# Loading wv in row blocks over two queues, and taking the v products of the first tiles block-complete

## The chip, the core and the metric

The kernel runs on one core of one Trainium2 chip. The metric is the device time in microseconds (us) of one execution; lower is better. The kernel before takes 220.84 us, the median of three runs (220.69, 220.84, 221.06).

## The reference, cut to what matters

The input x has 2048 rows of 512 numbers. It is normalised row by row, and the same normalised x feeds two branches whose results are added to x:

```python
xn = _layernorm(x)                       # no gain, no bias
q, k, v = split(xn @ wqkv)               # wqkv is 512 x 1536; 32 heads of 16
phi = concat(softmax(. @ w_phi), softmax(-(. @ w_phi)))      # for q and for k
o = (phi_q @ (phi_k^T v)) / (phi_q @ sum(phi_k) + 1e-6)      # per head
out = x + o @ wo + ((xn @ w_gate) * (xn @ w_up)) @ w_down    # inner width 1792
```

All inputs and the output are bf16. The change concerns v of the first 512 rows: `v = xn @ wv`, where wv is the last third (512 columns) of wqkv.

## The kernel before, in words

Rows of x are handled in 16 tiles of 128 rows; four tiles make a group of 512. wv lies in SBUF as four row blocks of 128 x 512 (`wv[:, c, :]`, 128 KB each); block c multiplies the 128 columns c of a tile, so a tile's v is four matmuls on TensorE (PE) that add up in one PSUM bank, one for each block, over the transposed tile (`xnT`) as the stationary operand. All matmuls of the start have 512 columns.

The order of the work on every engine is the order of the code (a manual schedule), and each engine works strictly in that order. The weights come by a list of transfers written out at the head of the kernel (lines 82 to 95): SyncE (SP) issues tile 0 of x, tile 2, wv blocks 0 and 1 in one transfer, wv blocks 2 and 3 in another, then the first 256 columns of the gate and up weights (`wg`, `wu`), `wphi`, the next 384 columns of `wg` and of `wu`, the transposed key weights (`wT2`), tiles 4 to 7 of x, and the rest. ScalarE (ACT) issues tiles 1 and 3 of x (lines 102 and 103). In the built program these transfers share eight semaphores that are handed out in turn, so a transfer is issued only after the one eight places before it (counted over both queues, in the order of the code) has landed. Before, `wphi` thus waits for tile 0, the second piece of `wg` for tile 2, the second piece of `wu` for wv blocks 0 and 1, `wT2` for tile 1, and tiles 4 to 7 for wv blocks 2 and 3.

The first four tiles are normalised in a special way, so that the start is short. For tile n, VectorE (DVE) sums the rows (`sum_of`, line 373; tile 1's sum is made on ACT, line 376), then writes 512 x minus the sum (`sub_sum`, line 337); the standard deviation is multiplied in only later, when v leaves PSUM (`first_v_out`, lines 361 and 363). `lt(n)` (lines 202 to 206) transposes the tile on PE with four matmuls of 128 columns against an identity and copies the result out of PSUM on ACT. `first_v(n, js)` (line 353, matmuls at line 236) makes the products of tile n with the wv blocks in js. Tiles 0 and 1 use the two banks that later hold the kv sums, tiles 2 and 3 ordinary banks (`pv`). `warm_up(k, reps)` (line 306) issues k matmuls on constants, of 128 x reps columns, which nothing reads.

Before, PE's order at the start (lines 380 to 397) is: ten constant matmuls, transposes of tiles 0 and 1, two constant matmuls of 512 columns, transposes of tile 2, then blocks 0 and 1 for tiles 0, 1 and 2 (six matmuls), transposes of tile 3, blocks 2 and 3 for tiles 0, 1 and 2 (six matmuls), all four blocks of tile 3. Then come three units of the gated branch (`ffn(3)`: four `g` matmuls at line 274, four `u` matmuls at line 278 each), `fold` (line 225), which multiplies the key weights by `w_phi` and needs `wT2` and `bd`, and from there the steady alternation of v, k, q, `ffn` and `kv`, the attention and the final products (`fin`, lines 290 and 293).

Of the kernel before, what the change touches and what calls it, by code (L numbers as in the profile page):

```python
# [8 lines left out]
BF16 = mybir.dt.bfloat16  # L9
F32 = mybir.dt.float32  # L10
AF = mybir.ActivationFunctionType
# [10 lines left out]
def kernel(  # L22
# [12 lines left out]
    nc = tc.nc  # L35
    P = 128
    S, D = A_x.shape[-2], A_x.shape[-1]
# [4 lines left out]
    DC = D // P  # L42
# [10 lines left out]
    consts = ctx.enter_context(tc.tile_pool(name="consts", bufs=1))  # L53
# [4 lines left out]
    wv = wpool.tile([P, DC, D], BF16)  # L58
# [9 lines left out]
    def dma_x(lo, hi, eng=nc.sync):  # L68
        eng.dma_start(out=xall[:, lo:hi, :], in_=x_view[:, lo:hi, :])
# [1 line left out]
    def dma_cols(eng, w, src, lo, hi, at=0):  # L71
        eng.dma_start(out=w[:, :, lo - at:hi - at], in_=src[:, lo:hi].rearrange("(c p) f -> p c f", p=P))

    def dma_wv(lo, hi):
        nc.sync.dma_start(out=wv[:, lo:hi, :],
                          in_=A_wqkv[lo * P:hi * P, 2 * D:3 * D].rearrange("(c p) f -> p c f", p=P))

    def dma_gu(lo, hi):
        dma_cols(nc.sync, wg, B_w_gate, lo, hi)
        dma_cols(nc.sync, wu, B_w_up, lo, hi)  # L80

    dma_x(0, 1)
    dma_x(2, 3)
    dma_wv(0, 2)
    dma_wv(2, DC)
    dma_gu(0, 2 * P)
    nc.sync.dma_start(out=wphi[:], in_=A_w_phi.rearrange("(c h) d f -> (h d) c f", c=DC))
    dma_gu(2 * P, 5 * P)
# [5 lines left out]
    nc.sync.dma_start(out=wd[:], in_=B_w_down.rearrange("(c p) d -> p c d", p=P))  # L94
    nc.sync.dma_start(out=wo[:], in_=A_wo.rearrange("(c p) n -> p c n", p=P))

    ET = mybir.EngineType
    ctx.enter_context(tc.manual_schedule(engines={ET.PE, ET.DVE, ET.Activation, ET.Pool, ET.SP}))
    ones = nc.const_aps.tensor(1.0, [P, P], BF16)
    first = consts.tile([P, 1], BF16)  # L100
    nc.scalar.activation(out=first[:], in_=ones[:, 0:1], func=AF.Exp, scale=1.0)
    dma_x(1, 2, nc.scalar)
    dma_x(3, 4, nc.scalar)
    ident = consts.tile([P, P], BF16)
    make_identity(nc, ident[:])
    mhalf = consts.tile([P, GT], F32)
# [38 lines left out]
    def bank(name, dt=F32, n=TT):  # L145
        return ps_s.tile([P, n], dt, name=name, tag="s")
# [55 lines left out]
    def lt(n, lo=0, hi=DC):  # L202
        tp = bank("tp", BF16).rearrange("p (c t) -> p c t", c=DC)
        for c in range(lo, hi):
            nc.tensor.transpose(out=tp[:, c, :], in_=xns[n][:, c * P:(c + 1) * P], identity=ident[:])  # L205
        nc.scalar.copy(out=xnT[:, lo:hi, n * P:(n + 1) * P], in_=tp[:, lo:hi, :])  # L206
# [27 lines left out]
    def proj(ps, n, w, js=range(DC)):  # L234
        for j in js:
            nc.tensor.matmul(ps, lhsT=xnT[:, j, n * P:(n + 1) * P], rhs=w[:, j, :],  # L236
                             start=(j == 0), stop=(j == DC - 1))
# [68 lines left out]
    def warm_up(k, reps=DC):  # L306
        for _ in range(k):
            nc.tensor.matmul(warm[:, 0:reps * P], lhsT=ones,
                             rhs=nc.const_aps.tensor(1.0, [P, reps * P], BF16), start=True, stop=True)
# [4 lines left out]
    with tc.tile_pool(name="ps_k", bufs=1, space=PSUM) as ps_k:  # L314
# [38 lines left out]
        def first_v(n, js):  # L353
            if n not in vps:
                vps[n] = kvbank[n][:] if n < 2 else bank("pv")
            proj(vps[n], n, wv, js)
# [23 lines left out]
        lt(0, 0, 2)  # L380
        lt(0, 2, DC)
        lt(1)
        warm_up(2)
        for n in (2, 3):
            sum_of(n)
            sub_sum(n, tots[n])
        lt(2)
        for n in range(3):
            first_v(n, (0, 1))
        lt(3)  # L390
        first_v(0, (2, 3))
        first_v(1, (2, 3))
        first_v(2, (2, 3))
        for n in (2, 3, 0, 1):
            stats_of(n)
            scales_of(n, float(D))
# [125 lines left out]
```

## Time and profile before

| what | value |
| --- | --- |
| median of three runs | 220.84 us (220.69 to 221.06) |
| the profiled execution's own time | 220.88 us |
| its span, first to last instruction | 219.1 us |
| PE busy | 215.2 us (98%) |
| DVE busy | 140.9 us (64%) |
| ACT busy | 89.4 us (41%) |
| GpSimd (POOL) busy | 74.1 us (34%) |
| moved by DMA | 19.91 MB, mean 91 GB/s |

The profile is one execution. Its span is 1.78 us shorter than that execution's own time; what lies around the span is taken as unchanged. In the rows, PE is the matmuls, PEld the loading of their stationary operands, SPq and ACTq the issuing of transfers. A busy time of PE includes the pipelined end of a matmul, so that single matmuls of 512 columns show 0.38 us though they follow one another about every 0.216 us (four of them take 0.86 us in the chain). A row of the timeline gives the start, the time covered, the engine, the line, the operation and how many of them; the chain that ended last gives start, length and what it consisted of. "To landing" counts from the start of an issue to the last part of the transfer.

### The profile page before, as it was taken

How to read it: one execution, taken by the hardware profiler on the slowest of the kernel's cores; microseconds unless marked ns; L12 is line 12 of the kernel's file. 1: busy time of each engine (PE TensorE's matmuls, PEld its weight loads, DVE VectorE, ACT ScalarE, POOL GpSimd, SP SyncE). 2: the span in 40 equal slices, each digit the busy share in tenths (PEclk: the TensorE clock that was granted, in tenths of full speed). 3: DMA queues.
4: the chain of work that ended last, by engine and by line, in shares of the span. 5: the costliest groups of instructions: out<-in, count | busy, mean ns of one | idle time of the engine just before them, and what ended most of it. 6: DMA issues, size and time to landing. Idle time of an engine off the chain costs nothing.

```text
span 219.1 us, 3493 instructions
## 1 busy us (share of the span) xinstructions
PE 215.2 (98%) x1294; PEld 103.1 (47%) x1294; DVE 140.9 (64%) x239; ACT 89.4 (41%) x159; POOL 74.1 (34%) x71
## 2 busy tenths in 40 slices
PE   8999999999999999999999999999999999999994
PEld 3444445454444444444544444444444444454443
DVE  4868867886598758567599773296655645454321
ACT  5545686569574875565435212141231322100000
POOL 2450843363358454636045333033123033000000
PEclk9999999999999999999999999999999999999999
DMA  6999995303202540202018455114431431612301
GB/s 193 276 298 372 373 242 50 75 0 51 48 0 49 51 85 11 48 3 48 1 37 102 80 112 114 42 24 96 96 75 24 96 72 27 97 48 72 74 24 48
DMA packets 48529, 19.91 MB, mean 91 GB/s; under 512 B 37504, under 2 KB 48512, under 8 KB 48512
## 3 DMA queue, kind: packets, MB, share of 16 engines
q1 hardware_dynamic: 48224, 19.42, 39.8%
q10 hardware_dynamic: 288, 0.26, 0.4%
q8 instruction: 10, 0.16, 0.4%
q14 instruction: 7, 0.06, 0.1%
HBM read 8.67 MB, written 2.10 MB: 49 GB/s over the span
## 4 chain that ended last, share of the span: by engine, by line
PE 96%; DVE 1%; DMA 1%; issue 0%
PE g L274 22%; PE fin L290 22%; PE u L278 22%; PE fin L293 6%; PE k L236 6%; PE q L236 6%; PE pv L236 6%; PE ab L461 2%; PE kv L330 2%; DMA xall<-in_A_x_dram 1%; PE kv L236 1%; DVE tot L373 1%; PE pq L225 1%; DVE xn L337 0%; PE tp L205 0%
## 5 line engine op out<-in xcount | busy, mean ns | idle before, releaser
L274 PE MATMUL g<-xnT,wg 128*128 128x512 bf16 x224 | 57.5, 379 | 0.0
L278 PE MATMUL u<-xnT,wu 128*128 128x512 bf16 x224 | 57.5, 379 | 0.0
L282 DVE TENSOR_TENSOR hT<-u,g_sb 128x512 bf16<-128x512 f32 x56 | 37.0, 666 | 24.4 <-PE u L278 16.2
L253 POOL TENSOR_TENSOR phiq<-e,rsum 128x1024 bf16<-128x1024 f32 x16 | 30.9, 1933 | 63.5 <-DVE rsum L251 56.0
L281 ACT CAST g_sb<-g 128x512 bf16<-128x512 f32 x56 | 32.8, 586 | 47.1 <-PE g L274 46.9
L249 DVE TENSOR_REDUCE sums<-e 128x64 f32<-128x1024 f32 x32 | 38.9, 1216 | 20.1 <-ACT e L246 20.1
L290 PE MATMUL fin<-wd,hT 128*128 128x512 bf16 (+2 forms) x238 | 51.2, 367 | 0.0
L253 POOL TENSOR_TENSOR phik<-e,rsum 128x1024 bf16<-128x1024 f32 x16 | 30.9, 1932 | 40.0 <-DVE rsum L251 37.9
L278 PEld LDWEIGHTS <-wu 128*128 128x128 bf16 x224 | 21.9, 98 | 26.4
L290 PEld LDWEIGHTS <-hT 128*128 128x128 bf16 x238 | 22.4, 98 | 24.8
L274 PEld LDWEIGHTS <-wg 128*128 128x128 bf16 x224 | 21.1, 98 | 24.0
L236 PEld LDWEIGHTS <-xnT 128*128 128x128 bf16 x192 | 17.5, 97 | 18.3 <-ACT xnT L206 0.3
L300 DVE TENSOR_TENSOR o_sb<-fin,xall 128x512 bf16<-128x512 f32 (+2 forms) x13 | 8.5, 651 | 20.5 <-PE fin L293 20.5
L251 DVE RECIPROCAL rsum<-sums 128x64 f32<-128x64 f32 x32 | 17.7, 553 | 3.1
L293 PE MATMUL fin<-wo,oT 128*128 128x512 bf16 (+2 forms) x68 | 16.6, 367 | 0.0
L236 PE MATMUL k<-W1k,xnT 128*128 128x512 bf16 x64 | 16.4, 379 | 0.0
L236 PE MATMUL q<-W1q,xnT 128*128 128x512 bf16 x64 | 16.4, 378 | 0.0
L245 ACT ACTIVATE e<-q 128x512 f32<-128x512 f32 x12 | 7.2, 597 | 22.2 <-PE q L236 22.2
L236 PE MATMUL pv<-wv,xnT 128*128 128x512 bf16 x56 | 14.4, 380 | 0.0
L474 DVE TENSOR_TENSOR otok<-ab,rden 128x512 bf16<-128x512 f32 x16 | 11.1, 691 | 0.6
L322 ACT CAST vt<-pv 128x512 bf16<-128x512 f32 x12 | 7.0, 587 | 10.0 <-PE pv L236 10.0
L153 DVE BATCH_NORM_STATS2 stats<-xall 128x6 f32<-128x512 bf16 x16 | 10.6, 664 | 0.0
(61 smaller groups left out, 130.9 us busy)
## 6 DMA issues: line engine op xcount, KB each, us to landing
out_dram<-o_sb SPq DMA_DIRECT2D x15, 128.0 KB, 2.0
wd<-in_B_w_down_dram SPq DMA_DIRECT2D x1, 1792.0 KB, 15.4
xall<-in_A_x_dram SPq DMA_DIRECT2D x1, 1024.0 KB, 11.4
wg<-in_B_w_gate_dram SPq DMA_DIRECT2D x1, 640.0 KB, 7.7
wu<-in_B_w_up_dram SPq DMA_DIRECT2D x1, 640.0 KB, 9.5
wv<-in_A_wqkv_dram SPq DMA_DIRECT2D x2, 256.0 KB, 4.2
xall<-in_A_x_dram SPq DMA_DIRECT2D x1, 512.0 KB, 4.2
wg<-in_B_w_gate_dram SPq DMA_DIRECT2D x1, 512.0 KB, 5.3
```

Source lines behind the costliest of these rows:

```text
L153: nc.vector.bn_stats(out=stats[:], in_=xall[:, n, :])
L236: nc.tensor.matmul(ps, lhsT=xnT[:, j, n * P:(n + 1) * P], rhs=w[:, j, :], start=(j == 0), stop=(j == DC - 1))
L249: nc.vector.tensor_reduce(out=sums[:], in_=ev, axis=AX.X, op=ALU.add)
L251: nc.vector.reciprocal(out=rsum[:].rearrange("p a b -> p (a b)"), in_=sums[:])
L253: nc.gpsimd.tensor_tensor(out=phi[:].rearrange("p g (x f) -> p (g x) f", f=DH), in0=ev, in1=rsum[:].to_broadcast((P, 2 * H, DH)), op=ALU.mult)
L274: nc.tensor.matmul(gps, lhsT=wg[:, c, f * P:(f + 1) * P], rhs=xnT[:, c, T * TT:(T + 1) * TT], start=(c == 0), stop=(c == DC - 1))
L278: nc.tensor.matmul(ups, lhsT=wu[:, c, f * P:(f + 1) * P], rhs=xnT[:, c, T * TT:(T + 1) * TT], start=(c == 0), stop=(c == DC - 1))
L281: nc.scalar.copy(out=g_sb[:], in_=gps)
L282: nc.vector.tensor_tensor(out=hTs[T][:, f, :], in0=ups, in1=g_sb[:], op=ALU.mult)
L290: nc.tensor.matmul(ps, lhsT=hTs[T][:, f, t4 * P:(t4 + 1) * P], rhs=wd[:, f, lo:lo + w], start=(f == 0), stop=False)
L293: nc.tensor.matmul(ps, lhsT=oTs[n][:, c, :], rhs=wo[:, c, lo:lo + w], start=False, stop=(c == DC - 1))
L474: nc.vector.tensor_tensor(out=o_tok[:].rearrange("p (b h d) -> p b h d", b=2, d=DH), in0=abv[:, :, :, 0:DH], in1=rden[:].to_broadcast((P, ...
```

## The change

wv comes as three transfers instead of two: block 0 and then blocks 2 and 3 on SyncE's queue, block 1 on ScalarE's, behind tiles 1 and 3 of x. The ScalarE lines are moved up in the code so that they stand before the gate and up weights. The two constant matmuls after the transposes of tile 1 shrink from 512 to 128 columns. PE's order becomes: all four blocks of tile 0, transposes of tile 2, all of tile 1, transposes of tile 3, all of tile 2, all of tile 3. The number of instructions is the same but for the one more transfer on ScalarE. In the built program the turn of the semaphores moves by one: the first piece of `wu` now waits for tile 0 of x, `wphi` for tile 2, the second piece of `wg` for wv block 0, the second piece of `wu` for tile 1, `wT2` for wv blocks 2 and 3, and tiles 4 to 7 for tile 3.

```diff
-    def dma_wv(lo, hi):
-        nc.sync.dma_start(out=wv[:, lo:hi, :],
+    def dma_wv(lo, hi, eng):
+        eng.dma_start(out=wv[:, lo:hi, :],
...
-    dma_wv(0, 2)
-    dma_wv(2, DC)
+    dma_wv(0, 1, nc.sync)
+    dma_wv(2, DC, nc.sync)
+
+    ET = mybir.EngineType
+    ctx.enter_context(tc.manual_schedule(engines={ET.PE, ET.DVE, ET.Activation, ET.Pool, ET.SP}))
+    ones = nc.const_aps.tensor(1.0, [P, P], BF16)
+    first = consts.tile([P, 1], BF16)
+    nc.scalar.activation(out=first[:], in_=ones[:, 0:1], func=AF.Exp, scale=1.0)
+    dma_x(1, 2, nc.scalar)
+    dma_x(3, 4, nc.scalar)
+    dma_wv(1, 2, nc.scalar)
     dma_gu(0, 2 * P)
...
-    ET = mybir.EngineType
-    ctx.enter_context(tc.manual_schedule(engines={ET.PE, ET.DVE, ET.Activation, ET.Pool, ET.SP}))
-    ones = nc.const_aps.tensor(1.0, [P, P], BF16)
-    first = consts.tile([P, 1], BF16)
-    nc.scalar.activation(out=first[:], in_=ones[:, 0:1], func=AF.Exp, scale=1.0)
-    dma_x(1, 2, nc.scalar)
-    dma_x(3, 4, nc.scalar)
...
         lt(1)
-        warm_up(2)
+        warm_up(2, 1)
+        first_v(0, range(DC))
         for n in (2, 3):
             sum_of(n)
             sub_sum(n, tots[n])
         lt(2)
-        for n in range(3):
-            first_v(n, (0, 1))
+        first_v(1, range(DC))
         lt(3)
-        first_v(0, (2, 3))
-        first_v(1, (2, 3))
-        first_v(2, (2, 3))
+        first_v(2, range(DC))
...
         first_v(3, range(DC))
```

More of the change, by code (lines that the diff above doesn't have):

```diff
@@ L72, in dma_cols @@
         eng.dma_start(out=w[:, :, lo - at:hi - at], in_=src[:, lo:hi].rearrange("(c p) f -> p c f", p=P))
-    def dma_wv(lo, hi):
-        nc.sync.dma_start(out=wv[:, lo:hi, :],
-                          in_=A_wqkv[lo * P:hi * P, 2 * D:3 * D].rearrange("(c p) f -> p c f", p=P))
+    def dma_wv(lo, hi, eng):
+        eng.dma_start(out=wv[:, lo:hi, :],
+                      in_=A_wqkv[lo * P:hi * P, 2 * D:3 * D].rearrange("(c p) f -> p c f", p=P))
     def dma_gu(lo, hi):
```

## The prediction

> **What bounds the kernel now.** I read the page first, then the chain that ended last, in order of time, over the part that the change touches, then the transfers of wv.
>
> ```profile
> span 219.1 us, 3493 instructions
> PE 215.2 (98%) x1294; PEld 103.1 (47%) x1294; DVE 140.9 (64%) x239; ACT 89.4 (41%) x159; POOL 74.1 (34%) x71
> PE 96%; DVE 1%; DMA 1%; issue 0%
> ```
>
> TensorE (PE) carries 96% of the chain. What is left is the start, before its first useful matmul. From there to the end each piece of work on PE follows the last, so whatever the start gains or loses is handed on unchanged to the end; nothing later absorbs it. The chain by time shows where PE becomes the bound:
>
> ```profile
> 5.39 0.37 DVE xn L337
> 5.76 0.05 issue
> 5.80 0.40 PE tp L205 x4
> 6.20 0.86 PE kv L236 x4
> 7.07 0.43 PE pv L236 x2
> 7.50 0.22 PE tp L205 x4
> 7.72 0.86 PE kv L236 x4
> 8.58 1.29 PE pv L236 x6
> 9.88 0.86 PE g L274 x4
> ```
>
> The columns are start, length, what. Up to 5.76 the chain runs over DVE, which prepares tile 2; from tile 2's transposes at 5.80 PE has no gap. (The chain counts a matmul's pipelined end, 0.17 us; in the timeline the same steps begin earlier, the v products at 6.04, the first `g` at 9.71. I use those starts.) One matmul of 512 columns costs 0.86 / 4 = 0.216 us, four transposes 0.22 us. Check: 6.04 + 16 x 0.216 + 0.22 = 9.72.
>
> So the only thing to win lies before 5.80:
>
> ```profile
> 4.36 0.86 PE L205 MATMUL tp<-ident,xn 128*128 128x128 bf16 x8
> 5.05 0.60 PE L308 MATMUL warm<-const-bfloat16-1.0 128*128 128x512 bf16 x2
> 5.80 0.40 PE L205 MATMUL tp<-ident,xn 128*128 128x128 bf16 x4 [0.15 <-DVE xn L337]
> ```
>
> Between 5.05 and 5.80 PE does nothing that is needed: two constant matmuls (2 x 0.216), then a wait for DVE. The change puts tile 0's v products there. Whether they can run depends on wv:
>
> ```profile
> L75 SPq DMA_DIRECT2D wv<-in_A_wqkv_dram x2: 430/450/469, 1.7 to 2.2; - x2
> DMA to landing us min/median/max: 4.0/4.2/4.3
> ```
>
> ```profile
> SPq L72 <- DMA wv<-in_A_wqkv_dram: 0.6, 1, 0.6
> ```
>
> The first line gives the issues' durations and their first and last start, the second the times to landing. SP's wait for a wv transfer ends when it issues `wu` at 5.77, and 1.71 + 4.0 = 5.71: that is blocks 0, 1. Blocks 2, 3 then have the 4.3: the two issues end at 1.71 + 0.94 = 2.65, the second starts at about 2.18, so these blocks land at **6.48**. Before, that is harmless: they are first needed at 7.56, behind tile 3's transposes, so 1.1 us of other work hides them.
>
> **The change, part by part.**
>
> PE's sum. Removed: 2 x 512 constant columns for 2 x 128, which end at about 5.05 + 0.11 = 5.16. Moved: all four products of tile 0 ahead of tile 2's transposes. Nothing needed is added or taken away. Tile 0's transposed halves are ready: ACT's copies begin at 4.68 and 4.95, at 0.37 each, so the second is out at about 5.3, before block 2 is needed. Queued on PE behind the product with block 2, call its landing T, are: that product and the one with block 3, tile 2's transposes, four products of tile 1, tile 3's transposes, four of tile 2, four of tile 3: 14 x 0.216 + 2 x 0.22 = 3.46 us. A wait costs 0.02 (tile 0 landed at 0.79 + 2.48 = 3.27, DVE began at 3.29). Hence the first `g` starts at **T + 3.48**, against 9.71: the change in time is **T - 6.23**. With T early, the floor is PE's own work: products with blocks 0 and 1 end at 5.16 + 0.43 = 5.59, so `g` starts at 9.05 and the most to gain is 0.66 us.
>
> The other waits in that chain hold. Blocks 0 and 1 landed together at 5.71 before; split over two queues neither should be later, and PE needs only 5.71 + 0.43 = 6.14 for both products at the latest, less than the T I take. Tile 2's copy on ACT (0.17 after its transposes, then 0.58) lies beside tile 1's products and tile 3's transposes (0.86 + 0.22), tile 3's 0.75 beside tile 2's 0.86. That cover is thin, 0.1 us; if it is gone it costs that much less than 0.1.
>
> When do blocks 2, 3 land? They are issued at the same place (2.15 instead of 2.18, since a 128-row issue takes 0.40 against 0.43) and the same bytes lie ahead: 512 KB of x, 256 KB of wv. What is new is that ScalarE's queue carries 384 KB of this, not 256. Bounds:
>
> ```profile
> 2.50:3.50 1.00, 1.00 (x4) 0.43 (x3) 0.21 (x1) 0.05 (x1) 0.00 (x0) 1.00 1.03 341
> 4.00:5.00 1.00, 0.92 (x11) 0.43 (x10) 0.98 (x4) 0.49 (x4) 0.00 (x0) 1.00 0.94 294
> ```
>
> The last column is GB/s. With both queues at work (2.5 to 3.5) 341 GB/s moved, with SP's alone (4 to 5) 294. If block 1 keeps both at work for 256 KB more, these take 0.77 us and not 0.89: T = 6.48 - 0.12 = **6.36**. That is the value I take, the nearest row with its one known difference. Lower end: the transfers of 5.5 to 6.0 are
>
> ```profile
> DMA packets 262, 0.14 MB, mean 285 GB/s; under 512 B 3, under 2 KB 262, under 8 KB 262
> ```
>
> about 530 bytes each, `wg`'s 512-byte rows and no longer wv's of 1 KB. The bulk of wv is thus through by about 5.6, and 6.48 is a laggard among the 16 engines. Without it T is 5.6 and the gain 0.63. Upper end: the transfer of the same size behind it needed longer,
>
> ```profile
> wg<-in_B_w_gate_dram SPq DMA_DIRECT2D x1, 256.0 KB, 4.7
> ```
>
> 2.18 + 4.7 = 6.88, a loss of 0.65.
>
> The Trainium skill, "DMA: Bandwidth & Descriptors", section "Issuing engines are not separate DMA queues", says that transfers issued by different engines run on the same 16 engines and interleave, and that several issuers save only issue time. By that rule T stays 6.48 and the time is 0.25 us longer, 221.13; the two rates above speak for a little more than that, the interleaving agrees.
>
> SP's other transfers. The shifted semaphores delay some: the second piece of `wg` now waits for block 0, which lands at 5.7 or earlier, so up to 1.4 us later than 4.30; it then lands at 5.7 + 5.5 = 11.2, and its first use is `g` at 13.17. The second piece of `wu` follows after 0.88, at 6.6 + 5.2 = 11.8 for 14.03. `wT2` waits for blocks 2, 3 and for these issues, 7.1 and not 6.35; it lands 6.3 later, at 13.4, against `fold` at 14.99. Everything on SP behind it slips by the same 0.8: tiles 4 to 7 land at 15.8, read at 18.18. All hidden, by 1.6 us or more; cost nothing, and nothing if PE comes 0.6 earlier. `fold` also needs `bd`, done on POOL at 13.6, untouched and 0.7 early even then. ScalarE's extra issue, 0.4 us at about 1.71, ends before its sum at 3.45. DVE is behind at first (its first `hT` at 11.93), but has 0.17 us to spare for each `ffn` unit (0.69 against 0.86 for one half of it), and the banks are free by then.
>
> Sum: 6.36 - 6.23 = +0.13 us on 220.88, the profiled execution's own time, which is 0.04 above the median of the runs: **221.0 us**. The slot before 5.80 is filled, but PE then stands before block 2 as long as it used to stand before tile 2.
>
> **Rivals.** What can be told from no change is 0.2%, 0.44 us; on the median that is below 220.40 or above 221.28.
>
> 1. *Forecast: PE waits for blocks 2, 3 until 5.75 to 6.62.* Change -0.48 to +0.39, 220.4 to 221.3. For it: the landing of 6.48 in the one execution shown. Chance 0.64.
> 2. *They come with the bulk.* If the laggard belongs to that execution only, T is at most 5.75 and the kernel gains 0.48 to 0.66: 220.3. For it: the packets of 5.5 to 6.0. Against: it needs all 16 engines in step, and x alone, issued from 0.79, took 2.5 to 2.8 with little ahead of it. Chance 0.14.
> 3. *They come later, slower than before.* One late engine now stops PE, where 1.1 us of cover hid it. It decides from T = 6.62; with `wg`'s 4.7 the time is 221.5. For it: `wg` itself; more in flight on ScalarE's queue when they start. Against: the bytes ahead are the same. Chance 0.18.
> 4. *PE's clock falls back while it waits.* The first constant matmuls follow each other every 0.43 us (weight loads at 1.21, 1.63, 2.06), from 4.36 on PE runs twice as fast, after some 3.5 us of work. The change leaves about 0.75 us without work (5.6 to 6.36). If it fell back for another 3.5 us, half of that is lost, 1.75: 222.8. Against: the idle 0.3 us of now and its wait for DVE did no harm. Chance 0.04. The Trainium skill, "TensorE: Matmul & The Clock Gate", section "What's actually happening", gives an idle window of about 3.4 us before the clock falls back; no run here shows it, and it is why I go no higher.
>
> **The numbers.** The likeliest is 221.0. Range: case 2's floor (220.88 - 0.63) and the upper end of T with 0.05 to spare give 220.3 to 221.6; only case 4 and the tails of 2 and 3 lie outside. Faster 0.14, within 0.2% 0.64, slower 0.18 + 0.04 = 0.22.
>
> **What would show it.** In the new profile: block 2's product starts within 0.05 of the landing of blocks 2, 3; PE's gap lies there and no longer before tile 2's transposes; the first `g` starts 3.48 after that landing; from there on every piece of PE is shifted by the same amount. I am wrong if the product of block 2 starts without a wait, if T lies outside 5.75 to 6.62, if blocks 0 or 1 come last, or if a gap opens at `fold` or at tile 4's v.

## The result

The changed kernel takes **221.64 us** (median of 22 executions, 220.82 to 223.27), the kernel before in as many 221.03 us: 0.6 us or 0.27% slower, ratio 1.0027, 95% interval 1.0016 to 1.0038. The forecast was 221.0, at most 221.6. So the sign of the forecast's +0.13 was right, the size was not: it came out as its third rival.

The profiled execution of the changed kernel is one of its faster ones, 221.16 us, span 219.4. Its chain in order of time, the same stretch as before:

```profile
4.56 1.07 PE tp L207 x8
5.62 0.21 PE warm L310 x2
5.84 1.22 PE kv L238 x4
7.06 0.22 PE tp L207 x4
7.28 0.86 PE kv L238 x4
8.14 0.22 PE tp L207 x4
8.37 1.73 PE pv L238 x8
10.09 0.86 PE g L276 x4
```

Tile 0's four products now stand ahead of tile 2's transposes, as the change says. They take 1.22 us where four should take 0.86, and the eight transposes 1.07 where they took 0.86: PE runs at half its rate up to about 6.4. The first `g` stands at 10.09 in the chain, 9.88 before (the chain counts a pipelined end of 0.17, so the forecast's T + 3.48 reads T + 3.65 here). The transfers of wv:

```profile
L75 SPq DMA_DIRECT2D wv<-in_A_wqkv_dram x2: 432/433/434, 1.7 to 2.2; - x2
L75 ACTq DMA_DIRECT2D wv<-in_A_wqkv_dram x1: 453/453/453, 1.7 to 1.7; - x1
...
DMA to landing us min/median/max: 3.0/4.1/4.2
```

Block 0 lands at 1.7 + 3.0 = 4.7, block 1 at 1.73 + 4.1 = 5.8, blocks 2 and 3 at 2.18 + 4.2 = 6.4, near the 6.36 of the forecast. The time of this execution, too, is near the forecast's sum, but that is luck: its chain has no wait for wv at all. At half rate block 1's product lasted until 6.46, so that block 2's product, which starts then, found its data landed. The forecast named just this, a product with block 2 that starts without a wait, as a sign of being wrong. Nor is the execution typical: the median is 0.5 above it. One number ties the profiles together: an execution's own time less the place of the first `g` in its chain is 211.0 before (220.88 - 9.88), 211.07 after, and 210.96 to 211.14 in all the profiles below. Everything happens ahead of the first `g`.

### The profile page after: what moved, and what is told of

It is laid out like the page before. It is cut to its first block, busy times and chain, and to the rows that moved or that the text cites. A ratio compares the mean times of both kernels' runs of the same rounds, so it can differ in the third digit from the quotient of the medians.

```text
span 219.4 us, 3470 instructions
## 1 busy us (share of the span) xinstructions
PE 214.1 (98%) x1270; PEld 103.5 (47%) x1294; DVE 140.9 (64%) x239; ACT 89.6 (41%) x159; POOL 74.2 (34%) x71
## 4 chain that ended last, share of the span: by engine, by line
PE 96%; DMA 1%; issue 1%; DVE 1%
PE g L276 22%; PE u L280 22%; PE fin L292 22%; PE fin L295 6%; PE q L238 6%; PE k L238 6%; PE pv L238 6%; PE ab L461 2%; PE kv L332 2%; DMA xall<-in_A_x_dram 1%; PE kv L238 1%; PE tp L207 1%; PE pq L227 1%; DVE tot L375 0%; DVE xn L339 0%
## 5 line engine op out<-in xcount | busy, mean ns | idle before, releaser
L276 PE MATMUL g<-xnT,wg 128*128 128x512 bf16 x215 | 56.5, 379 | 0.5
L280 PE MATMUL u<-xnT,wu 128*128 128x512 bf16 x220 | 56.8, 379 | 0.2
L238 PE MATMUL k<-W1k,xnT 128*128 128x512 bf16 x60 | 15.7, 379 | 0.1
L155 DVE BATCH_NORM_STATS2 stats<-xall 128x6 f32<-128x512 bf16 x16 | 10.6, 664 | 0.0
```

Source lines behind the costliest of these rows:

```text
L155: nc.vector.bn_stats(out=stats[:], in_=xall[:, n, :])
L276: nc.tensor.matmul(gps, lhsT=wg[:, c, f * P:(f + 1) * P], rhs=xnT[:, c, T * TT:(T + 1) * TT], start=(c == 0), stop=(c == DC - 1))
L280: nc.tensor.matmul(ups, lhsT=wu[:, c, f * P:(f + 1) * P], rhs=xnT[:, c, T * TT:(T + 1) * TT], start=(c == 0), stop=(c == DC - 1))
```

## The experiments

Two theories. **W**: PE waits for wv's blocks 2 and 3, and these land later in most executions than in the first two profiles. **C**: PE's clock rises later, or falls back, because the change leaves PE with less to do between 5.1 and 6.4 us. All ratios are to the kernel before on the same chip, which had medians of 220.95 to 221.11. One execution of e1 (463 us) and one of e13 (809 us) were disturbed; they are left out of the ranges and counts, and leaving them out of the medians too would move these by less than 0.05. The upper group, below, is the executions over 222.5 us, the lower group all others; the kernel before has none over 221.7.

### Constants, transfers and order taken apart

e1, the changed kernel with `warm_up(2)` for `warm_up(2, 1)`:

> The changed kernel with the two constant matmuls after tile 1's transposes back at 512 columns. Theory C (the clock): in the changed kernel's profile PE still runs at half rate until about 6.4 us (the four transposes' rows are 0.107 us apart, the first v products 0.43), in the profile before only until about 4.3. The loss comes from that, because PE has less to do between 5.1 and 6.4 us and its clock rises later in a part of the executions. Then the wider constants, which end before blocks 2 and 3 of wv have landed (6.37), take most of the loss back: 221.1 us, ratio 0.9995 to 1.0010 to the kernel before, and the slow tail over 222 us is gone. Theory W (the wait): PE waits for blocks 2 and 3 of wv, which on most executions land later than in the one profiled (about 6.8). Then nothing changes: 221.6 us, ratio about 1.0027.

Measured: 221.46 us (221.24 to 221.88), ratio 1.0017, interval 1.0007 to 1.0027. Nearer to W, though the interval reaches into C's range too. Its profile (221.88 us) shows the wait bare; PE was at full rate from about 5:

```profile
2.18 4.97 DMA wv<-in_A_wqkv_dram
7.15 0.04 issue
7.20 0.59 PE kv L238 x2
7.79 0.22 PE tp L207 x4
8.01 0.86 PE kv L238 x4
8.87 0.22 PE tp L207 x4
9.10 1.73 PE pv L238 x8
10.82 0.86 PE g L276 x4
```

The chain no longer runs over DVE: it goes from the issue of blocks 2 and 3 at 2.18 through their landing at 7.15 into the product with block 2 (the x2 are blocks 2 and 3 of tile 0). 7.15 + 3.65 = 10.80, and `g` stands at 10.82. The changed kernel as it is does the same in an execution near its median (e13's profile, 221.57 us):

```profile
2.18 4.69 DMA wv<-in_A_wqkv_dram
6.87 0.04 issue
6.91 0.59 PE kv L238 x2
```

6.87 + 3.65 = 10.52, and its first `g` stands at 10.54.

e2, the kernel before with `warm_up(2, 1)` for `warm_up(2)`:

> The kernel before with the two constant matmuls cut from 512 to 128 columns, and nothing else. Tile 2's transposes still wait for VectorE until 5.80. Theory C: PE has 0.3 to 0.6 us less work ahead of 5.8, so its clock rises later in a part of the executions: 221.2 to 221.6 us, ratio 1.0005 to 1.0025, and a wider spread. Theory W: no change, ratio within 0.0005 of 1.

Measured: 221.10 us (220.69 to 221.46), ratio 0.9997, interval 0.9988 to 1.0007. Short constants alone cost nothing that can be told; C fails here, for the kernel before.

e3, transfers changed, order kept:

> Only the three transfers of wv and the shifted semaphores are changed, PE's order is that of the kernel before. Both theories: blocks 2 and 3 are needed at 7.56 us and have landed; ratio within 0.0005 of 1. If it is slower by 0.3 us or more, the transfers themselves (a later tile 0, a later weight) carry the loss, which neither theory says.

Measured: 221.19 us (220.96 to 221.52), ratio 1.0004, interval 0.9996 to 1.0013: no difference that can be told. The transfers and the shifted semaphores do not carry the loss.

e4, order changed, transfers kept:

```diff
-        warm_up(2)
+        warm_up(2, 1)
+        first_v(0, range(DC))
...
         lt(2)
-        for n in range(3):
-            first_v(n, (0, 1))
+        first_v(1, range(DC))
         lt(3)
-        first_v(0, (2, 3))
-        first_v(1, (2, 3))
-        first_v(2, (2, 3))
+        first_v(2, range(DC))
```

> PE's new order, with its short constant matmuls, on the two wv transfers of the kernel before: blocks 0 and 1 land at about 5.7 instead of 4.8 and 5.8, blocks 2 and 3 at 6.5. Theory C: PE stands idle longer ahead of block 0, the clock rises later still: 221.7 to 222.3 us, ratio 1.003 to 1.006, with a wide spread. Theory W: blocks 2 and 3 land as late as in the changed kernel or 0.1 later: 221.6 to 221.7 us, ratio 1.0027 to 1.003, with no wider spread.

Measured: 222.12 us (221.10 to 223.39), ratio 1.0046, interval 1.0024 to 1.0068. Two groups: seven executions from 221.1 to 222.3, five from 223.0 to 223.4. The median and the wide spread are what C had forecast, the lower group by itself (median 221.58) what W had; two separate groups neither had. In the upper group's profile (223.17 us) the four products of tile 1 take 1.71 us and not 0.86: half rate up to about 10 us.

### The wait taken away

e5, tiles 0 and 1 multiply by data that have long landed:

```diff
-            proj(vps[n], n, wv, js)
+            for j in js:
+                nc.tensor.matmul(vps[n], lhsT=xnT[:, j, n * P:(n + 1) * P], rhs=wv[:, j, :] if n >= 2 else xall[:, 0, :],
+                                 start=(j == 0), stop=(j == DC - 1))
```

> The changed kernel, but the v products of tiles 0 and 1 take tile 0 of x (landed at about 3.3 us) as their moving operand in place of every block of wv, so v of these two tiles is left out and something else of the same size computed. Nothing else is changed; wv's blocks 2 and 3 are first needed by tile 2, at about 7.7 us. Theory W (PE waits for wv, which lands at 6.4 to 7.2 from execution to execution): the wait is gone, the first g starts at 9.1 to 9.4, the time is 220.3 to 220.6 us, ratio 0.9965 to 0.998. Theory C (PE's clock rises later, whatever the transfers do): without a wait PE has also no idle time, so the tail over 222 us goes, but with the short constants the median stays over 221.2.

Measured: 220.63 us (220.32 to 221.85), ratio 0.9986, interval 0.9973 to 0.9999, about 1 us below the changed kernel and a little above W's 220.3 to 220.6; C's median over 221.2 fails. Its profile (220.32 us):

```profile
5.17 0.12 PE warm L310 x2
5.28 0.86 PE kv L359 x4
6.14 0.22 PE tp L207 x4
6.37 0.86 PE kv L359 x4
7.23 0.22 PE tp L207 x4
7.45 1.73 PE pv L359 x8
9.18 0.86 PE g L276 x4
```

No gap anywhere, `g` at 9.18: the forecast's floor was 9.05 + 0.17 = 9.22. In this execution blocks 2 and 3 landed at 2.17 + 4.8 = 7.0, which would have put `g` at 10.6. So PE's new order does what it says; wv comes too late for it. The edit takes away the waits for all blocks of wv; that blocks 2 and 3 end the last of them is read from the chains of e1 and e13. W holds for the lower group.

### More profiles of both kernels

> The changed kernel once more, for a second profile. W: blocks 2 and 3 land at 6.6 to 7.1 and the product with block 2 starts within 0.05 of that, the first g 3.48 later, 10.1 to 10.6; time 221.4 to 221.9. C: PE's rows are at half rate until after block 2 has landed, and the first g comes later than landing plus 3.48.

> The changed kernel, a third profile. Blocks 2 and 3 at 6.6 to 7.1; the product with block 2 within 0.05 of that, the first g 3.48 later unless PE's granted clock is down, in which case it is over 0.3 later still: 221.4 to 221.9 us without, over 222.5 with.

> The kernel before once more, for a second profile. If late landings are the rule and the first profile was lucky, blocks 0 and 1 land at 5.8 to 6.4 and blocks 2 and 3 at 6.6 to 7.2; the first product then starts within 0.05 of blocks 0 and 1, the first g 3.68 later, and the late blocks 2 and 3 cost nothing: 220.9 to 221.4 us.

> The kernel before, a third profile: as for the second, 220.9 to 221.4 us, blocks 2 and 3 landing at 6.5 to 7.2 without a wait of PE for them.

e11 (the changed kernel, 221.53 us): blocks 2 and 3 at 6.8, `g` at 10.49 in the chain, 6.8 + 3.65 = 10.45. e10 and e12 (the kernel before, 221.47 and 221.17 us): blocks 2 and 3 at 6.9 and 6.7, with no wait of PE for them, as expected. What I had not expected: e10's time is 0.07 above its range, and in both the first product starts at 6.5 and 6.3, 0.3 behind blocks 0 and 1 (landed at 6.2 and 6.0), because tile 2's transposes came late. e10 shows why, and with it what spreads the kernel before:

```profile
5.40 0.85 PE warm L308 x2
6.25 0.43 PE tp L205 x4
6.68 1.00 PE kv L236 x4
...
10.49 0.86 PE g L274 x4
```

Its two constant matmuls took 0.85 us and tile 2's transposes 0.43, twice their usual time, and the first four products 1.00 where four take 0.86: half rate up to about 6.8, and `g` at 10.49 instead of 9.88. So the time of the clock's rise differs from execution to execution, in both kernels.

Over all 18 profiles of this study blocks 2 and 3 land between 6.4 and 7.3, the median at 6.9. The two with which I began, 6.5 and 6.4, are the two earliest. On two queues they come no earlier than on one: 6.4 to 7.2 in the ten profiles with block 1 on ScalarE's queue, 6.5 to 7.1 in the six with the old transfers, medians within 0.1 (e9 and e16, which read another matrix, not counted). With this scatter a gain of 0.1 could hide, but none is seen.

e8 (the changed kernel, 223.41 us) is in the upper group, and shows why. Here the clock did not rise late, as e8's expectation had it under C; it rose early and fell again. The stretches, with PEclk, the granted clock, as the third column from the right:

```profile
3.67:7.08 3.41, 2.11 (x16) 0.97 (x15) 3.30 (x9) 1.78 (x5) 0.00 (x0) 1.00 0.99 275
7.08:10.49 3.41, 3.40 (x15) 1.73 (x15) 2.85 (x9) 0.58 (x1) 2.26 (x6) 0.50 1.11 287
10.50:12.00 1.50, 1.50 (x10) 0.60 (x8) 1.34 (x2) 0.98 (x2) 1.32 (x6) 1.00 1.18 200
```

The first number behind the length is PE's busy time: 2.11 of 3.41 us. Then the granted clock is 0.50 for 3.41 us, and 1.00 again. The chain of the same execution:

```profile
2.18 4.87 DMA wv<-in_A_wqkv_dram
7.05 0.04 issue
7.09 1.01 PE kv L238 x2
8.10 0.43 PE tp L207 x4
8.53 1.71 PE kv L238 x4
10.23 0.41 PE tp L207 x4
10.64 1.73 PE pv L238 x8
12.37 0.86 PE g L276 x4
```

Blocks 2 and 3 land at 7.05, so W alone gives 10.70; the half rate adds 1.67: `kv` x4 takes 1.71 and not 0.86, each row twice its length until 10.5.

### The clock: filling and emptying the wait

e6 is e4 with `warm_up(3)` for its `warm_up(2, 1)`:

> PE's new order on the old two transfers of wv (222.12 us, 5 of 12 executions between 223.0 and 223.4, its profile with PE at half rate until 10.1 us), with three constant matmuls of 512 columns instead of two of 128 ahead of tile 0's products. They end at 5.7 to 6.35, about when blocks 0 and 1 land. Theory C for the upper group: PE's idle time between 5.4 and 6.2 keeps the clock low for one more window; filled, no execution is over 222.3 and the median is 221.5 to 221.7. Theory W for what is left: PE still waits for blocks 2 and 3, so it does not come back to 221.05. If the group at 223 stays, the clock does not depend on this idle time.

Measured: 221.52 us (221.20 to 221.80), ratio 1.0015, interval 1.0007 to 1.0024; none of 11 in the upper group, against 5 of 12 in e4 (on another chip). C for the upper group, W for the lower.

The same on one chip for the changed kernel itself: e13 is unchanged, e14 has `warm_up(4)`, e15 no constants there.

> The changed kernel, on the same chip as the three runs that follow, as their measure. C: a lower group at 221.1 to 221.9 and, in 1 of 10 executions or more, an upper group at 222.5 to 223.5.

> The changed kernel with four constant matmuls of 512 columns in place of two of 128. They end at 5.9 (full rate) to 6.8 (half rate), that is before or about when blocks 2 and 3 land. C for the upper group: no execution over 222.3. W for the lower group: the median stays at 221.4 to 221.7, since PE still waits for blocks 2 and 3. If the upper group stays, PE's load in this stretch does not decide it.

> The changed kernel without the two short constant matmuls. C: 0.1 to 0.2 us less work in the stretch, so at least as many executions in the upper group as the changed kernel has on the same chip; the lower group within 0.1 of the changed kernel's, since the product with block 2 waits for its transfer anyway.

| | upper group (over 222.5 us) | median of all, us | ratio, interval |
| --- | --- | --- | --- |
| e14, four long constants | 0 of 12 | 221.74 | 1.0024, 1.0014 to 1.0035 |
| e13, two short ones | 0 of 11 | 221.54 | 1.0016, 1.0004 to 1.0028 |
| e15, none | 5 of 12 | 221.76 | 1.0048, 1.0025 to 1.0070 |

Without constants the upper group is there, with four long ones it is not. Between e13 and e14 this table shows no difference: e13 had none, against what I expected. All the changed kernel's runs together have 3 of 35 (222.92, 223.27 and e8's 223.41); with longer constants (e1 and e14) it is 0 of 22, too few to tell from 3 of 35. Over both sets of transfers, the versions with longer constants (e1, e6, e14) have 0 of 33, the two with the new order, the old transfers or no constants (e4, e15) 10 of 24. e14's median is a little above the 221.4 to 221.7 expected; the intervals of e13 and e14 overlap. In e14's profile four long constants at half rate outlast the landing (the last starts at 6.61). e15's profile (223.24 us) has another form of the slow start, a clock that rises late and has not fallen before:

```profile
1.71 4.44 DMA wv<-in_A_wqkv_dram
6.15 0.04 issue
6.19 2.05 PE kv L238 x4
8.24 0.43 PE tp L207 x4
8.67 1.57 PE kv L238 x4
...
12.18 0.86 PE g L276 x4
```

PE is idle until block 0 lands at 6.15, and works at half rate until about 10. PEclk reads 1.00 in this stretch, though the rows are twice their length; so a late rise can be read from the rows alone.

### Two that failed

e7, wv's first blocks ahead of tiles 2 and 3 of x:

```diff
     dma_x(0, 1)
+    dma_wv(0, 1, nc.sync)
     dma_x(2, 3)
-    dma_wv(0, 1, nc.sync)
...
     dma_x(1, 2, nc.scalar)
+    dma_wv(1, 2, nc.scalar)
     dma_x(3, 4, nc.scalar)
-    dma_wv(1, 2, nc.scalar)
...
-        first_v(0, range(DC))
+        first_v(0, (0, 1))
...
         lt(2)
-        first_v(1, range(DC))
+        first_v(1, (0, 1))
+        first_v(2, (0, 1))
         lt(3)
-        first_v(2, range(DC))
+        for n in range(3):
+            first_v(n, (2, 3))
```

> A version for both theories: wv block 0 goes ahead of tile 2 of x on SyncE's queue and block 1 ahead of tile 3 on ScalarE's; PE's order is that of the kernel before, but with tile 0's products with blocks 0 and 1 ahead of tile 2's transposes (and the short constants). Blocks 0 and 1 should land at 4.0 to 4.9, blocks 2 and 3 at 6.4 to 7.2 as before, needed at about 7.5. W: PE is bound from 5.80 with two products fewer to do, but waits about 0.3 us for tile 2's copy: 220.7 to 220.9 us, ratio 0.9985 to 0.9995. If tile 2 of x comes later than 4.7 for it, the gain is lost and the ratio is 1.0 to 1.002. C: no group over 222, since the products themselves fill the time from 5.2 to 5.6.

Measured: 222.38 us (221.38 to 224.08), ratio 1.0061, interval 1.0034 to 1.0089, the slowest but for e9, below. What was won on wv is lost on x:

```profile
1.71 4.26 DMA xall<-in_A_x_dram
5.97 0.02 issue
5.99 0.70 DVE tot L375
...
7.13 0.41 PE tp L207 x4
```

Tile 2 lands at 5.97, so its transposes start at 7.13 and not 5.80. Two of the eight executions were near 224; no profile shows one of these, so whether the clock is the reason there too stays open. Both forecasts for this version failed: the ratio of 1.0 to 1.002 for a late tile 2, and no execution over 222, which six of the eight are.

e9 and e16, the same kernel: what makes blocks 2 and 3 late? In most profiles the rate sags between 4.0 and 4.5 us (last column, GB/s), here the second one of the kernel before (e10),

```profile
4.00:4.50 0.50, 0.46 (x5) 0.16 (x3) 0.50 (x3) 0.15 (x2) 0.00 (x0) 1.00 0.70 207
```

against the first:

```profile
4.00:4.50 0.50, 0.42 (x5) 0.13 (x3) 0.48 (x3) 0.17 (x2) 0.00 (x0) 1.00 0.93 297
```

> The changed kernel with the three transfers for wv reading the matrix wo (512 x 512, its rows of 1 KB lie one behind the other) and not the last third of wqkv (rows of 1 KB, 3 KB apart). So v is left out and another product of the same size computed; sizes, queues and order are the same. What is tested is why blocks 2 and 3 land late: in several profiles the transfer rate drops between 4 and 5 us, when wv's rows are on their way, and single rows take 0.4 to 1.4 us instead of 0.05. Theory R (the drop comes from how wv's rows lie in memory): it goes, blocks 2 and 3 land at 5.6 to 6.2, the time is 220.4 to 220.9 us, ratio 0.997 to 0.999. Theory Q (it comes from the transfers' number or place in time): blocks 2 and 3 land at 6.4 to 7.2 as ever, 221.4 to 221.8 us, ratio 1.0015 to 1.0035.

> The changed kernel with wv's transfers reading wo (v is left out, another product of the same size is computed): 4 of its 7 executions were in the upper group. If that was the chip or chance, its share is now like the changed kernel's beside it (1 or 2 of 10); if what is read decides it, it is again a half or more.

Measured, e9: 223.10 us (221.11 to 223.27), ratio 1.0074, interval 1.0047 to 1.0101, blocks 2 and 3 at 7.1. e16: 221.74 us (221.29 to 223.54), ratio 1.0040, interval 1.0019 to 1.0060, blocks 2 and 3 at 7.2. Theory R falls: how wv's rows lie in memory is not the reason. What makes the rate sag stays open, and the sag between 4.0 and 4.5 alone does not set the landing: e5 and e13 have none (285 and 301 GB/s) and land at 6.95 and 6.87, e3 has one (240) and lands at 6.62. The share of the upper group was 4 of 7 in e9 and 3 of 12 in e16, one and the same kernel on two chips; with so few executions the two do not differ clearly.

## Why the prediction was wrong, step by step

- **PE hands on every delay.** Right. First `g` plus 211.0 to 211.1 gives every profile's time, so nothing behind it absorbs or adds anything.
- **The first `g` starts at T + 3.48.** Right wherever PE waited at full rate: e1, e11, e13, and e6 (landing 6.89, `g` in the chain at 10.56, expected 10.54). In the changed kernel's first profile PE did not wait for block 2, so that one says nothing for it.
- **T = 6.36, from one landing and a gain by the second queue.** This step failed, and it is the term of the sum that was mis-sized: the mechanism, PE waiting before block 2, was right. The landing of 6.48 was one draw, and an early one; the median of 18 profiles is 6.9, and the changed kernel's own four profiles have 6.4, 6.8, 6.9 and 7.05. The forecast called the late engine's part "a laggard" and asked whether it would go away (rival 2) or grow (rival 3). The packets of the traces show two other things. In every profile the landing comes 0.4 us (0.39 to 0.46) after the last row of wv has ended, in the first one at 6.5 after 6.1; so T could not be the time at which the bulk is through. And a late landing is not one straggler: at 5.5 us 24 and 38 of wv's 512 rows were still to end in the two profiles with which I began, 57 to 162 in the others (e7, where rows of x are among them, aside). The second queue's 0.12 is not seen either. By the forecast's own formula 6.9 gives 220.88 + 6.9 - 6.23 = 221.55; measured were 221.64 and, in e13, 221.54. The right price stood in the text, under rival 3 with a chance of 0.18.
- **The rule of the Trainium skill on issuing engines** ("DMA: Bandwidth & Descriptors", "Issuing engines are not separate DMA queues"). The traces agree with it rather than with the step that I took from two stretches of different rates: medians within 0.1 us with one queue and with two, though the scatter is too wide to exclude 0.12.
- **Blocks 0 and 1 by 5.71.** Too early as well: 5.8 to 6.5 for block 1 in the changed kernel's four profiles. It costs the lower group nothing, since blocks 2 and 3 are later still.
- **The rest of SP's list is hidden.** Right: e3, and the same 211.0 to 211.1 behind the first `g` in all profiles. `wT2` was issued between 6.39 and 7.12 in the changed kernel's four profiles (6.35 before; 7.1 was allowed).
- **Rival 4, the clock.** The price was right (1.75 forecast, 1.67 measured in e8), the chance of 0.04 perhaps too low: it came in 3 of 35 executions of the changed kernel, and in 5 of 12 with fewer constants (e15). I leaned on the Trainium skill ("TensorE: Matmul & The Clock Gate", "What's actually happening"), which gives an idle window of about 3.4 us before the clock falls back. The length recurs here, in a half-rate stretch of 3.41 us in e8, but the condition does not: PE was busy 2.11 of the 3.41 us ahead of it. The measurement decides.
- **The kernel before as the measure.** Its 220.88 was also a good draw; the median went from 220.84 (three runs) to 221.03 (22). Two things can put it later: the clock, which rose late in e10 and e12 and on which their chains run, and blocks 0 and 1, for which the first product waits in e2 (the kernel before but for its short constants; landing 6.37, first product 6.41). How much each has in the median is not shown. The change still loses, because it moves what lands last, at 6.9, from a place with cover (needed at 7.56) to one without.

## What to carry to other kernels

Before work is moved ahead into a gap, take the landing of its data from several executions: one landing is a draw (6.4 to 7.3 us here), and it comes 0.4 us behind the last row. A transfer whose landing scatters belongs behind work that covers the scatter; taking one of the four blocks to a second queue did not visibly bring it forward. A gap ahead of PE's first long stretch can cost more than its length, since the clock can stay at half, or fall to it, for 3.4 us. Short of useful work, longer constant matmuls in the gap went with no slow execution here (0 of 33 over 222.5 us, against 10 of 24 in e4 and e15); the wait itself they left.

## What the runs showed of the hardware

- PE's granted clock fell to 0.50 after a stretch of 3.41 us with 2.11 us of PE work in it, and rose again 3.41 us later (e8). e16's profile shows the same: 1.92 us busy between 3.73 and 7.14, then 0.50. What the limit is stays open: in e7 PE was busy 1.91 us between 5.07 and 8.48 and the clock stayed at 1.00.
- With the same ten constants at the head of the kernel (seven of 512 columns, three of 128), PE reaches full rate anywhere between 3.7 and 6.8 us in sixteen of the 18 profiles (3.7 in e8, 4.1 before, 5.0 in e1, 6.1 in e12, 6.4 after, 6.8 in e10), and only at 10.0 and 10.1 in e15 and e4.
- The rate of the transfers sags to 135 to 264 GB/s between 4.0 and 4.5 us in 14 of the 18 profiles (285 to 322 in the other four), from 328 or more between 3.0 and 3.5, and the two profiles with the rows one behind the other are among the 14 (264 in e9, 174 in e16).
- The landing of wv's last blocks comes 0.39 to 0.46 us after the last row of wv has ended, in all 18 profiles.
